# Three more leaves of a weight gradient computed by pairs, and the input sums of its fourth combination made and stored in the first convolution

## The chip, the cores and the metric

The kernel runs on one core of a Trainium2 chip. Its engines are TensorE (matmuls; PE in the profile, and PEld for the loading of its stationary operand), VectorE (DVE), ScalarE (ACT), GpSimd (POOL) and SyncE (SP). Each engine works through its own list of instructions in order. Nearly all DMAs are issued by SP, also in order. The metric is device microseconds of one execution, lower is better. The kernel before takes 1146.25 us, the median of 3 runs (1141.46 to 1150.02).

## The reference

The reference is the forward pass and the gradient of a strided convolution over time, followed by a normalization of each channel over time and a GELU:

```
B, T, D, K = 2, 16000, 256, 31          # bf16
s = 2;  L = (T - K) // s + 1            # 7985
h = sum over i < K of  x[:, i:i + s*L:s, :] @ w[i]
mu, var = mean and variance of h over time, for each channel
h = (h - mu) / sqrt(var + 1e-5) * gn_gamma + gn_beta
out = gelu(h)                           # tanh form
returns out and the gradients by x, w, gn_gamma, gn_beta for a given grad_out
```

So there are three large pieces of matmul work: the forward convolution, the gradient by x, and the gradient by w (31 matrices of 256x256, each a sum over 2 x 7985 time steps).

## The kernel before

**The five stages.** F0 and F1 are the forward convolution of the first and of the second of the two sequences (b = 0, 1), each in four chunks of time (c = 0 to 3). Beside F1, and beside the stage after it, DVE and ACT do the GELU and its derivative. G0 and G1 are the gradient by x. W is the gradient by w, the last stage, from about 818 us to the end. In F0, DVE and SP also build transposed and summed copies of w for later (`w2_part`, once in each chunk).

**Fewer products.** Every convolution is split by even and odd taps into two levels of a three-product scheme: each level replaces four products by three, at the price of sums and differences of the inputs, which DVE makes. The letters A, B_, C_ name the three branches of a level. In W the two outer levels give nine combinations, n = 0 to 8, in the order of `COMBOS`: (A,A), (A,C), (A,B), (C,B), (B,B), (B,A), (B,C), (C,A), (C,C). A letter B_ in the table means that the raw input blocks of two phases are added, so a combination with one B_ needs sums of two blocks of x, and (B,B) sums of four.

**One combination of W.** Its inputs are four tiles of x (two sequences, two phases k3; 128 partitions x 8 x 512) and tiles of the incoming gradient, which earlier stages left in DRAM (`dld`). A third level gives three leaves: the middle one, A and C_. The middle leaf is always done "by pairs", a fourth level of the same scheme: `pair_x` adds neighbouring x blocks (DVE, L1564 or L1568), `w_pairs` multiplies the sums (PE, 16 matmuls of 256 columns for each half h), `pair_d` makes two differences of the gradient (DVE, L1584), and `w_single` multiplies those by single blocks (32 matmuls of 256 columns for each half). A leaf A or C_ is done in one of two ways. If (n, leaf) is in the set `NODES`, it is done by pairs too, with `pair_x`, `pair_d` and, for each half, `w_both` (DVE, L1608), which adds the pair product to the partial sums in PSUM. Otherwise `w_leaf` does it straight: 32 matmuls of 512 columns for each half, with nothing for DVE to prepare. All matmuls of W are recorded under one line, L1498. `leaf_d` (DVE, L1669) makes the differences of the gradient for A and C_ in every combination.

**The x tiles.** There are two sets of four SBUF tiles, used by even and odd n in turn. `x_tile(n)` fills the set of combination n while n - 1 is being multiplied. Where one raw block is wanted, it is a load of 1 MB. For n = 2 and n = 4 the tiles of the two sets are added in place (`w_add`, L1463, 128x4096). For n = 3, 5 and 6 two raw blocks are to be added: the first is loaded straight into the tile, and for the other `x_more` loads two pieces of 512 KB and adds each on DVE (`w_add`, L1463, 128x2048), eight adds in one combination.

**What sets the order.** The kernel first records every operation with its dependences, and then issues all of them in the order of one long table of numbers, `SEQUENCE`, which is part of the source. So the place of an operation on its engine is given by that table, not by where it stands in the code. The table is different whenever the list of operations is.

**The buffers that matter here.** Pair sums and differences live in buffers `PD` that are used in turn: two sets for n = 2, one for n = 3 and n = 5, two for n = 8. In F0 the area of `w2_part` (`VR` and `VD`, 14 KB in each partition) holds one quarter of w at a time; its results are stored to DRAM by SP. The transposed chunk of x that F0 works on has one buffer only, so the four transposing DMAs of the next chunk (L349) can start only when the sums of the present one are made, and the next chunk's first sums on DVE (L506) wait for them.

Of the kernel before, what the change touches and what calls it, by code (L numbers as in the profile page):

```python
# [34 lines left out]
def mmt(n):  # L35
# [229 lines left out]
def conv_stem_kernel(  # L265
# [1476 lines left out]
    for b, c, br in fw:  # L1742
# [7 lines left out]
        if b == 0 and br == C_:  # L1750
            plan.hold = plan.npe
            w2_part(c)
            plan.hold = -1
# [77 lines left out]
```

## Time and profile before

| what | before |
|---|---|
| median of 3 runs | 1146.25 us (1141.46 to 1150.02) |
| the profiled execution | 1140.03 us |
| its span from first to last instruction | 1138.2 us |
| mean granted TensorE clock | 0.997 |
| PE busy | 1108.9 us, 97% |
| DVE busy | 1010.8 us, 89% |
| ACT busy | 558.7 us, 49% |
| POOL busy | 133.5 us, 12% |
| DMA | 243.56 MB, mean 214 GB/s |

The profile comes from one execution, which was 6 us below the median. In it 1.8 us lie outside the span. PE is busy nearly all of the time in every stage, with small waits for the most part; DVE is second. The views used below are the page's table of engines, the groups of instructions by line and shape, the waits, the busy time of each engine in stretches of time, and the instructions in order of time.

### The profile page before, as it was taken

What the parts mean: (1) busy time and instruction counts of PE and PEld (TensorE: products, weight loads), DVE (VectorE), ACT (ScalarE), POOL (GpSimd) and SP (SyncE); (2) the same over time, 40 slices, a digit from 0 to 9 for tenths busy, and PEclk for the clock granted to TensorE, in tenths of its full rate; (3) what the DMA queues carried; (4) which work ended last, traced back from release to release, by engine and by line L of the source; (5) the groups of instructions that cost most, each with busy time, mean ns of one, the idle gap of its engine ahead of it and who ended that gap; (6) DMA issues with size and microseconds to landing.
All of it is one profiled execution on the core that took longest, in us unless ns stands there. A gap on an engine that the chain in (4) does not pass through costs nothing. (4 is left out here: it accounts for less than half of the span.)

```text
span 1138.2 us, 18913 instructions
## 1 busy us (share of the span) xinstructions
PE 1108.9 (97%) x7592; PEld 742.6 (65%) x7592; DVE 1010.8 (89%) x1013; ACT 558.7 (49%) x826; POOL 133.5 (12%) x212
## 2 busy tenths in 40 slices
PE   7999999999999999999999999999899999999998
PEld 5888899877777974444444444444488666666785
DVE  7998687688989999899999989988999998788895
ACT  1253444487887579777867667565212212121200
POOL 0000000000000032423221332332100000000000
PEclk9999999999999999999999999999999999999999
DMA  9648827859696699999966697899997926999575
GB/s 222 97 129 137 208 84 162 202 134 214 174 229 156 202 390 250 287 262 252 265 184 173 172 224 199 196 222 229 300 292 238 299 99 191 332 328 305 187 188 144
DMA packets 358037, 243.56 MB, mean 214 GB/s; under 512 B 234167, under 2 KB 327613, under 8 KB 355773
## 3 DMA queue, kind: packets, MB, share of 16 engines
q1 hardware_dynamic: 350845, 223.47, 74.5%
q0 software_dynamic: 7104, 18.89, 5.8%
q8 instruction: 59, 0.97, 0.3%
q14 instruction: 29, 0.24, 0.1%
HBM read 106.24 MB, written 80.25 MB: 164 GB/s over the span
## 5 line engine op out<-in xcount | busy, mean ns | idle before, releaser
L548 PE MATMUL ps<-arena 128*128 128x256 bf16 (+4 forms) x3460 | 407.2, 281 | 9.9 <-DMA arena<-in_x_dram 5.2
L1232 PE MATMUL ps<-arena 128*128 128x512 bf16 (+1 forms) x1812 | 393.5, 379 | 11.5 <-DVE ps L1309 4.4
L548 PEld LDWEIGHTS <-arena 128*128 128x128 bf16 x3460 | 337.8, 98 | 79.4 <-DMA arena<-in_x_dram 5.5
L1232 PEld LDWEIGHTS <-arena 128*128 128x128 bf16 x1812 | 178.0, 98 | 225.0 <-issue 19.0
L1498 PE MATMUL ps<-arena 128*128 128x256 bf16 (+1 forms) x2320 | 309.5, 296 | 4.3 <-DMA arena<-dld 1.2
L1498 PEld LDWEIGHTS <-arena 128*128 128x128 bf16 x2320 | 226.9, 98 | 87.3 <-issue 4.1
L643 ACT ACTIVATE arena<-ps 128x1024 f32<-128x1024 f32 x124 | 125.6, 1023 | 256.9 <-PE ps L1498 83.6
L506 DVE TENSOR_TENSOR arena<-arena 128x2080 bf16<-128x2080 bf16 (+8 forms) x125 | 154.9, 1264 | 26.9 <-PE ps L548 26.3
L344 POOL DMA_DIRECT2D dld<-arena x144 | 104.0, 724 | 249.1 <-DMA arena<-arena 231.0
L923 DVE TENSOR_TENSOR arena<-arena 128x2048 bf16<-128x2048 bf16 (+1 forms) x80 | 95.5, 1196 | 6.2 <-ACT arena L917 2.6
L1463 DVE TENSOR_TENSOR arena<-arena 128x4096 bf16<-128x4096 bf16 (+1 forms) x50 | 87.3, 1772 | 6.7 <-DMA arena<-in_x_dram 3.8
L1309 DVE TENSOR_TENSOR ps<-ps,arena 128x1024 f32<-128x1024 f32 x60 | 72.3, 1225 | 8.5 <-PE ps L1232 5.3
L1180 DVE TENSOR_TENSOR arena<-arena 128x1032 bf16<-128x1032 bf16 (+1 forms) x110 | 72.0, 688 | 3.4 <-PE ps L1232 2.8
L663 ACT ACTIVATE arena<-ps 128x512 bf16<-128x512 f32 (+1 forms) x64 | 37.1, 581 | 55.9 <-PE ps L548 50.4
L1600 ACT COPY ps<-ps 128x256 f32<-128x256 f32 x54 | 19.2, 362 | 79.7 <-PE ps L1498 78.7
L353 POOL MEMSET arena<- 128x128 bf16 (+9 forms) x31 | 8.5, 297 | 403.9 <-DVE arena L506 257.6
L1319 DVE TENSOR_TENSOR arena<-ps,arena 128x1024 bf16<-128x1024 f32 x40 | 48.5, 1217 | 6.0 <-PE ps L1232 4.9
L618 ACT ACTIVATE arena<-ps 128x512 f32<-128x512 f32 x56 | 29.5, 602 | 38.6 <-PE ps L548 30.9
L1584 DVE TENSOR_TENSOR arena<-arena 128x2048 bf16<-128x2048 bf16 x36 | 43.2, 1216 | 2.8 <-PE ps L1498 2.3
L1669 DVE TENSOR_TENSOR arena<-arena 128x4608 bf16<-128x4608 bf16 x16 | 40.5, 2549 | 3.2 <-PE ps L1498 3.2
L584 ACT ACTIVATE ps<-ps 128x256 f32<-128x256 f32 x72 | 26.6, 370 | 33.5 <-PE ps L548 32.2
L913 DVE SCALAR_TENSOR_TENSOR arena<-arena 128x2048 bf16<-128x2048 bf16 (+1 forms) x16 | 35.8, 2237 | 6.7 <-ACT arena L910 6.5
(89 smaller groups left out, 791.4 us busy)
## 6 DMA issues: line engine op xcount, KB each, us to landing
arena<-in_x_dram SPq DMA_DIRECT2D x28, 1024.0 KB
dld<-arena POOLq DMA_DIRECT2D x144, 128.0 KB, 3.8
out_dram<-arena SPq DMA_DIRECT2D x31, 512.0 KB
arena<-in_x_dram SPq DMA_DIRECT2D x26, 512.0 KB
arena<-hd SPq DMA_DIRECT2D x24, 512.0 KB
arena<-dld SPq DMA_DIRECT2D x18, 640.0 KB
arena<-dld SPq DMA_DIRECT2D x18, 576.0 KB
vl<-arena SPq DMA_DIRECT2D x36, 256.0 KB
```

The costliest lines, as they stand in the source:

```text
L344: lambda: e.dma_start(out=out, in_=in_), dma=np_ * ns / 16e3 * 1.03, ns=ns, tp=SH[pk], slack=slack)
L506: lambda: nc.vector.tensor_tensor(out=o, in0=a, in1=b, op=ALU.add))
L548: yield nc.tensor.matmul(ps[:, dh, cs], lhsT=wt, rhs=mv, start=s0, stop=False, skip_group_check=True)
L643: lambda: nc.scalar.activation(out=out, in_=ps, func=ACT.Copy, scale=scale))
L923: add("DVE", dve(nf), [o], [a, b_], lambda: V.tensor_tensor(out=o, in0=a, in1=b_, op=op))
L1180: lambda: nc.vector.tensor_tensor(out=o, in0=a, in1=b, op=ALU.subtract))
L1232: yield nc.tensor.matmul(ps[:, e, 0:wide], lhsT=lt, rhs=mv, start=s0, stop=False, skip_group_check=True)
L1309: lambda ps=ps, g=g: nc.vector.tensor_tensor(out=ps[:], in0=px[:], in1=g, op=ALU.add))
L1319: lambda: nc.vector.tensor_tensor(out=ho[:, :, k, :], in0=ps[:], in1=g, op=ALU.add))
L1463: add("DVE", dve(o.free_size()), [o], [a, b], lambda: nc.vector.tensor_tensor(out=o, in0=a, in1=b, op=ALU.add))
L1498: yield nc.tensor.matmul(ps[:, s, c0:c1], lhsT=lt, rhs=mv, start=s0, stop=False, skip_group_check=True)
L1584: add("DVE", dve(2048), [o], [u, v], lambda o=o, u=u, v=v: nc.vector.tensor_tensor(out=o, in0=u, in1=v, op=ALU.subtract))
```

## The change

Two things are changed, and the order table is a new one.

First, `NODES` gains three entries: leaf A and leaf C_ of n = 2, combination (A,B), and leaf A of n = 8, combination (C,C). They are now done by pairs.

Second, the x tiles of n = 3, combination (C,B), are no longer added up in W. A new function `x_sums` does it in F0, in the first sequence's chunks 0, 1 and 2, for one, one and two of the four tiles: it loads two raw blocks in pieces of 512 KB into the area that `w2_part` uses, adds them on DVE, and stores the sum to new DRAM tiles `xs_d`. In W, `x_tile(3)` only loads them back, in two pieces of 512 KB for each tile.

```diff
 SEQUENCE = (
-    6, 11, 8, 7, 12, 5, 3, 10, 21, 15, 1, 16, 4, 2, 14, 13, 36, 34, 31, 39, 18, 30, 33, 40,
...
 )
...
+    xs_d = [[dram.tile([P, 2, 2048], BF16, name=f"xsd{b}_{k}") for k in range(2)] for b in range(NB)]
...
-    NODES = {(0, A), (0, C_), (1, A), (1, C_), (3, A), (4, A), (6, A), (7, A), (7, C_), (8, C_)}
+    NODES = {(0, A), (0, C_), (1, A), (1, C_), (3, A), (4, A), (6, A), (7, A), (7, C_), (8, C_), (2, A), (2, C_), (8, A)}
...
+    def x_sums(b, k3):
+        q = [sb(REG + 4096 * i, 4, 512) for i in range(3)]
+        for j, f in enumerate((0, 4)):
+            u, v = q[2 * j], q[1]
+            load(u, xblk(b)[:, f:f + 4, 4 * k3 + 2, :], 1 << 19, 1024)
+            load(v, xblk(b)[:, f:f + 4, 4 * k3, :], 1 << 19, 1024)
+            w_add(u, u, v)
+            load(xs_d[b][k3][:, j], u.rearrange("p f c -> p (f c)"), 1 << 19, 4096)
+
     def x_tile(n, b, k3):
...
+        elif (i1, i2) == (C_, B_):
+            for j in range(2):
+                load(t[:, 4 * j:4 * j + 4].rearrange("p f c -> p (f c)"), xs_d[b][k3][:, j], 1 << 19, 4096)
         else:
...
         if b == 0 and br == C_:
             plan.hold = plan.npe
             w2_part(c)
+            for k in ((0,), (1,), (2, 3), ())[c]:
+                x_sums(*KEYS[k])
             plan.hold = -1
```

The first place where the new order matters is DVE in combination n = 2 of W. Each row is one or more instructions in a line of the program; the line is that of the helper. In the kernel before, from the `pair_d` of the middle leaf; some rows towards the end belong to n = 3 already: L1584 is `pair_d`, L1669 `leaf_d`, L1463 `w_add` (128x4096: sums of whole tiles; 128x2048: the pieces of `x_more`), L1568 `pair_x`, L628 the last sums of n = 2.

```order
L1584 TENSOR_TENSOR arena<-arena 128x2048 x2
L1669 TENSOR_TENSOR arena<-arena 128x4608 x2
L1463 TENSOR_TENSOR arena<-arena 128x2048 x4
L1463 TENSOR_TENSOR arena<-arena 128x4096
L1584 TENSOR_TENSOR arena<-arena 128x2048 x2
L1568 TENSOR_TENSOR arena<-arena 128x2048
L1463 TENSOR_TENSOR arena<-arena 128x4096
L1463 TENSOR_TENSOR arena<-arena 128x2048 x2
L1463 TENSOR_TENSOR arena<-arena 128x4096
L1463 TENSOR_TENSOR arena<-arena 128x2048 x2
L1463 TENSOR_TENSOR arena<-arena 128x4096
L628 TENSOR_TENSOR arena<-ps,arena 128x1024 x3
```

In the changed kernel the same helpers stand some lines lower: L1684 is `leaf_d`, L1599 `pair_d`, L1583 `pair_x`, L1623 `w_both`, L1466 `w_add`, L631 the last sums.

```order
L1684 TENSOR_TENSOR arena<-arena 128x4608
L1599 TENSOR_TENSOR arena<-arena 128x2048
L1684 TENSOR_TENSOR arena<-arena 128x4608
L1583 TENSOR_TENSOR arena<-arena 128x2048 x3
L1599 TENSOR_TENSOR arena<-arena 128x2048 x3
L1623 TENSOR_TENSOR ps<-ps,arena 128x1024
L1599 TENSOR_TENSOR arena<-arena 128x2048
L1623 TENSOR_TENSOR ps<-ps,arena 128x1024 x3
L1466 TENSOR_TENSOR arena<-arena 128x4096 x2
L1583 TENSOR_TENSOR arena<-arena 128x2048
L1599 TENSOR_TENSOR arena<-arena 128x2048
L631 TENSOR_TENSOR arena<-ps,arena 128x1024
```

The eight adds of 128x2048 of `x_more` are gone from here, and `pair_x`, `pair_d` and `w_both` of the two leaves of n = 2 have come; `w_both` writes PSUM that matmuls are waiting to add to.

The second place is SP in F0, between chunk 2 and the transposing DMAs that fetch the first chunk of the second sequence. In the kernel before (`vl` are the stores of `w2_part`, `hd` that of the forward result):

```order
L344 DMA vl1_58<-arena_118 128x2x512 x2
L349 DMA_TRANSPOSE arena_118<-in_x_dram 128x8x272
L344 DMA hd0_2_62<-arena_118 128x4096
L344 DMA vl2_59<-arena_118 128x2x512
L349 DMA_TRANSPOSE arena_118<-in_x_dram 128x8x272 x3
```

In the changed kernel (`in_x_dram 128x4x512` are the loads of `x_sums`, `xsd` its stores):

```order
L347 DMA vl1_58<-arena_122 128x2x512
L347 DMA arena_122<-in_x_dram 128x4x512 x3
L347 DMA vl0_57<-arena_122 128x2x512
L347 DMA xsd1_1_101<-arena_122 128x2048
L347 DMA vl2_59<-arena_122 128x2x512
L347 DMA arena_122<-in_x_dram 128x4x512
L352 DMA_TRANSPOSE arena_122<-in_x_dram 128x8x272
L347 DMA arena_122<-in_x_dram 128x4x512 x2
L352 DMA_TRANSPOSE arena_122<-in_x_dram 128x8x272
L347 DMA xsd1_1_101<-arena_122 128x2048
L347 DMA hd0_2_62<-arena_122 128x4096
L347 DMA arena_122<-in_x_dram 128x4x512 x2
```

The loads and stores of the sums now stand before and between the four transposing DMAs of that chunk; the last two of them come after the rows shown, behind one more store of a sum, which itself waits for DVE.

287 rows, old and new, of the table SEQUENCE are left out of this document.

## The prediction

> **What bounds the kernel now.** I read the page's table and chain first, then the busy time by stretches, then the waits of PE and DVE in W, and last the groups by shape.
>
> ```profile
> span 1138.2 us, 18913 instructions
> PE 1108.9 (97%) x7592; PEld 742.6 (65%) x7592; DVE 1010.8 (89%) x1013; ACT 558.7 (49%) x826; POOL 133.5 (12%) x212
> PE 35%; DVE 4%; DMA 3%; issue 1%; ACT 0%; SPq 0%; DVEq 0%; ACTq 0%; POOLq 0%
> ```
>
> PE is idle for 29.3 us in all (1138.2 - 1108.9), and the part of the chain that could be followed is PE's in the main. So matmul time taken away counts almost in full, as long as DVE keeps up. The stretches below are, in this order, three of F0, and of W: n = 0 and 1, n = 2, n = 3, n = 4 to 6, n = 7, n = 8. Columns: length; busy us (instructions) of PE, PEld, DVE, ACT, POOL; granted clock, DMA share, GB/s.
>
> ```profile
> 60.00:100.00 40.00, 39.85 (x365) 35.45 (x363) 35.09 (x34) 19.58 (x43) 0.00 (x0) 1.00 0.62 140
> 100.00:140.00 40.00, 40.00 (x368) 35.72 (x366) 31.54 (x28) 17.09 (x39) 0.95 (x1) 1.00 0.76 168
> 140.00:200.00 60.00, 60.00 (x584) 56.86 (x582) 49.08 (x42) 29.00 (x72) 0.91 (x2) 1.00 0.55 127
> 826.00:887.40 61.40, 59.83 (x545) 53.08 (x543) 60.92 (x44) 12.79 (x19) 0.35 (x1) 1.00 0.85 258
> 887.40:925.60 38.20, 38.17 (x225) 22.00 (x226) 35.61 (x25) 5.50 (x10) 0.00 (x0) 1.00 0.61 203
> 925.60:961.50 35.90, 35.08 (x258) 24.94 (x257) 32.59 (x21) 6.76 (x11) 0.00 (x0) 1.00 0.54 174
> 961.50:1069.10 107.60, 107.60 (x736) 72.03 (x737) 92.33 (x68) 19.89 (x32) 0.00 (x0) 1.00 0.85 284
> 1069.10:1101.30 32.20, 31.59 (x289) 28.15 (x288) 29.15 (x23) 4.03 (x8) 0.00 (x0) 1.00 0.72 236
> 1101.30:1135.00 33.70, 33.23 (x242) 23.40 (x240) 25.00 (x21) 2.14 (x6) 0.53 (x1) 1.00 0.71 160
> ```
>
> In W PE is full throughout. DVE is full too in n = 0 and 1 (60.92 of 61.40) and has 2.6 us to spare in n = 2. Its slack in W is 309.0 - 275.6 = 33.4 us, and the waits, from 826 us on, say of what kind it is:
>
> ```profile
> PE ps L1498 <- DVE arena L1568: 1.1, 2, 0.6
> PE ps L1498 <- DVE ps L1608: 0.8, 2, 0.5
> PE ps L1498 <- DVE arena L628: 0.6, 1, 0.6
> PE ps L1498 <- ACT ps L1600: 0.5, 1, 0.5
> ...
> DVE arena L1527 <- PE ps L1498: 8.9, 5, 7.4
> DVE ps L1608 <- PE ps L1498: 8.5, 2, 8.0
> DVE arena L628 <- PE ps L1498: 3.2, 1, 3.2
> DVE arena L1669 <- PE ps L1498: 3.2, 1, 3.2
> ```
>
> PE waited 3.0 us in all of W, five times of six for DVE. DVE waited for PE in few long pieces, 8.0 us in n = 4 and 7.4 us near the end: there it had run ahead. So W is bound by PE with DVE close behind, and from n = 0 to n = 2 the two are level.
>
> **The change part by part.** These are the groups of W that the change touches (busy us, mean ns):
>
> ```profile
> L1498 PEld LDWEIGHTS <-arena 128*128 128x128 bf16 x2287 | 223.6, 98 | 84.8 <-issue 2.6 <-DVE arena L1568 1.7
> L1498 PE MATMUL ps<-arena 128*128 128x256 bf16 x1776 | 197.2, 273 | 3.0 <-DVE arena L1568 1.1 <-DVE ps L1608 0.8 <-DVE arena L628 0.6
> L1498 PE MATMUL ps<-arena 128*128 128x512 bf16 x512 | 112.6, 379 | 0.0
> L1584 DVE TENSOR_TENSOR arena<-arena 128x2048 bf16<-128x2048 bf16 x36 | 43.2, 1216 | 2.8 <-PE ps L1498 2.3 <-DMA out_dram<-arena 0.5
> L1568 DVE TENSOR_TENSOR arena<-arena 128x2048 bf16<-128x2048 bf16 x29 | 34.9, 1217 | 0.6 <-PE ps L1498 0.4
> L1463 DVE TENSOR_TENSOR arena<-arena 128x2048 bf16<-128x2048 bf16 x24 | 28.5, 1216 | 0.5 <-DMA arena<-in_x_dram 0.5
> L1608 DVE TENSOR_TENSOR ps<-ps,arena 128x1024 f32<-128x1024 f32 x20 | 24.1, 1224 | 8.7 <-PE ps L1498 8.5
> ```
>
> *PE.* The mean is a matmul's latency; what it takes of PE in a stream is busy time by count: 112.6/512 = 220 ns at 512 columns, 197.2/1776 = 111 ns at 256. A straight leaf is 64 of the first, 14.1 us; a leaf by pairs is 32 (`w_pairs`) and 64 (`w_single`) of the second, 10.7 us. The stretch of n = 2 checks it: 96 of 256 and 128 of 512 columns make 38.8 us, and PE was busy for 38.17, so I take 2% off. Three leaves: 3 x 3.4 x 0.98 = **10.0 us less**, all on the path.
>
> The Trainium skill speaks against such a change. In "TensorE: Matmul & The Clock Gate", section "Back-to-back issue gap", a sustained stream of weight loads and matmuls is put at about 81 ns at N = 128 and about 131 ns at N = 512, so a narrow matmul costs far more than its share. By that page, 256 columns lying by a straight line at about 98 ns (my estimate), a leaf would go from 8.4 to 9.4 us and the three leaves would cost 3 us. The trace disagrees: 220 and 111 ns, nearly the ratio of the widths.
>
> *DVE.* Consecutive instructions overlap a little, so I take what one moves the next by:
>
> ```profile
> 887.30 2.35 DVE L1584 TENSOR_TENSOR arena<-arena 128x2048 bf16<-128x2048 bf16 x2
> ...
> 889.57 5.02 DVE L1669 TENSOR_TENSOR arena<-arena 128x4608 bf16<-128x4608 bf16 x2
> ...
> 894.51 7.02 DVE L1463 TENSOR_TENSOR arena<-arena 128x2048 bf16<-128x2048 bf16 x5
> ```
>
> Two adds of 2048 take 2.27 us (889.57 - 887.30), 1.13 each, and two of 4608 take 4.94; `w_both` counts as 1.13, and an add of 4096 as 2.2, between them by size. A leaf by pairs adds two each of `pair_x`, `pair_d` and `w_both`: 6.8 us, 20.4 for three. Eight `x_more` adds leave n = 2: 9.1 us less. In W DVE has 11.3 us more to do in 10 us less: 286.9 of 299, or 96%.
>
> What PE then waits I get by adding up, along the two lists, DVE's pieces up to the last one that a matmul needs, against PE's pieces before it (16 matmuls of 256 columns as 1.75 us, of 512 as 3.45), both from the first `w_single` of n = 0. At the first `w_pairs` of n = 2 DVE was 61.5 us along and PE 59.4: 2.1 us late. In the new list it is 62.8 against 59.4, 3.4 us late, and it stays so up to the first matmul of n = 3's straight leaf (106.5 against 103.1) and to the start of n = 4. After that DVE has slack again. So DVE costs PE 1.3 us more there. In n = 7 and 8 DVE has 54.2 + 6.8 = 61.0 us of work in 65.9 - 3.3 = 62.6, with chains from the last `w_single` over a sum, `pair_d` and `w_both` (3.4 us) covered by two `w_pairs` (32 x 111 ns = 3.6 us): I take 1 us. Together **2.3 us of new waits**. The lower bound is none; the upper, all 11.3 us of DVE's work, is the first rival.
>
> *F0.* The eight adds (9.1 us of DVE) go into the first 200 us; the three stretches above leave DVE 24.3 us there. SP gets 16 loads and 8 stores of 512 KB, 12.6 MB in all. The quickest long stretch moved 284 GB/s, so that is 44 us of the DMA engines, where 0.62, 0.76 and 0.55 of their time is used in 140 us: 52 us are free. Behind the loads and stores on SP stand the next chunk's transposing DMAs, and behind these DVE's sums L506 and so PE. The cover:
>
> ```profile
> 90.84 6.98 SPq L349 DMA_TRANSPOSE arena<-in_x_dram  x2
> ...
> 102.72 1.23 DVE L506 TENSOR_TENSOR arena<-arena 128x2064 bf16<-128x2064 bf16 x1
> ...
> 172.84 11.34 SPq L349 DMA_TRANSPOSE arena<-in_x_dram  x3
> ...
> 192.60 1.23 DVE L506 TENSOR_TENSOR arena<-arena 128x2064 bf16<-128x2064 bf16 x1
> ```
>
> The last transposing DMA was issued at 97.8 and its data used at 102.7; at the next edge but one, 184.2 and 192.6. That is 4.9 and 8.4 us, less the landing. A piece of 512 KB takes 1.8 us at 284 GB/s; the order puts the pieces between the transposes, but starts chunk 2's transposes earlier in PE's work than before. I take **0.5 us**; the bounds are 0 and the second rival.
>
> *With one answer.* The x loads of n = 3 fall from 8.4 to 4.2 MB in a stretch at 203 GB/s: hidden before, hidden now, and nothing waits for them in W but the adds. The `keep` copies of n = 2 on ACT go elsewhere in the same number. The remaining waits outside W (some 25 us, with the start) belong to an order that is new everywhere; nothing says better or worse, and I give them 0 with 4 us to both sides.
>
> **Sum.** -10.0 + 2.3 + 0.5 = -7.2 us. The profiled execution (1140.03, of it 1.8 us outside the span) becomes 1132.8. It stood 6.2 us under the median, so the same step from 1146.25 gives 1139.0.
>
> **The rivals.**
>
> *DVE becomes the bound of W.* If DVE's waits for PE are the price of its order and not slack, W grows by DVE's 11.3 us rather than shrinking: 1157.6; at half of that, 1152. For it: 60.92 of 61.40 in n = 0 and 1, and n = 2 now asks 35.6 + 13.6 - 9.1 = 40.1 us of DVE for 31.5 of PE. Against: the longest wait, 8.0 us, lies in n = 4, where delayed work can go. It decides if PE's waits in n = 2 and 3 pass 7 us.
>
> *The sums' traffic holds up the transposes in F0.* This one ends slower. Chunk 0 and chunk 1 get six pieces each, chunk 2 twelve: 11, 11 and 22 us of DMA at 1.8 us. If all of it stands ahead of the transposes, the covers of 4.9, 4.9 and 8.4 us leave 6 + 6 + 13 = 25 us of PE waiting at the edges: 1146.25 - 7.7 + 25 = 1163.5. It pays for the whole gain once a third of that comes true. For it: the order of SP, pieces between the transposes of the second sequence's first chunk. Against: free DMA time, and the earlier start.
>
> *All of it, and no new wait.* The adds leave n = 2 early enough, PE's old waits shrink, the new order is better elsewhere by some us: 1146.25 - 10.0 - 3.0 = 1133.
>
> *Weight loads set the pace of narrow matmuls.* Then a pair leaf pays for 96 loads of 98 ns instead of 64: +3.1 us, 9.4 us for three, 1155.7. The trace speaks against it with 111 ns for a matmul and its load together. The rule of the Trainium skill quoted above points the same way, and by its figures the time would be 1149.
>
> *The change does nothing on the path.* That would need another engine to end W; PE's 33.23 of 33.70 us in the last stretch excludes it nearly.
>
> **How the numbers follow.** My forecast has a chance of 0.54 (1135 to 1146), all of it and more 0.24, DVE as the bound 0.11, the traffic 0.08, weight loads 0.02, nothing 0.01. The predicted time is 1139. The runs of before spread by 4 us to either side of the median, so about 1% is what can be told from no change. The range goes from 1129 (all of it, less that spread) to 1153 (DVE as the bound at half, and the edge of the traffic). Faster by over 1% is below 1134.8: 0.24 and the lower edge of the forecast, 0.28. Slower by over 1% is above 1157.7: most of the traffic, the upper end of DVE as the bound, some of the weight loads, 0.12. Within 1%: 0.60.
>
> **What would show it.** Right: in W 192 fewer matmuls of 512 columns and 288 more of 256, still near 220 and 111 ns; PE's waits in W at about 5 us, the new ones in n = 2 and 3 for L1583, L1599 or L1623; F0 without a PE wait over 1 us between 70 and 200 us. Wrong: PE waits over 7 us in n = 2 and 3 (first rival), waits on L506 or a transposing DMA at the chunk edges (second), or a 256-column matmul above 120 ns. The prediction fails as a whole if a wait outside W, made by the new order, is larger than 7 us.

## The result and the profile after

The changed kernel takes **0.9931 of the time before, 95% interval 0.9913 to 0.9949**: 1136.01 us, the median of 14 runs (1132.57 to 1141.19), against 1144.04 us (14 runs, 1141.22 to 1150.02). That is 0.7% faster, within the 1% that the forecast had as likeliest. The forecast of 1139.0 stood on a median of three runs, 1146.25, which was itself 2.2 us above the later one. The profiled execution takes 1133.30 us, of it 1131.5 in the span; before it was 1140.03. So 6.7 us are gone there, where the prediction had 7.2. The page of the kernel after:

```profile
span 1131.5 us, 19151 instructions
PE 1097.4 (97%) x7642; PEld 751.2 (66%) x7688; DVE 1029.5 (91%) x1031; ACT 557.3 (49%) x826; POOL 135.9 (12%) x212
PE 21%; DVE 10%; DMA 3%; issue 2%; SPq 1%; ACT 0%; POOL 0%; DVEq 0%; ACTq 0%; POOLq 0%
```

PE is busy for 11.5 us less, DVE for 18.7 us more, and DVE's part of the chain has gone from 4 to 10%. (46 matmul records are missing from this trace: there are 7688 weight loads and 7642 matmuls.)

To see where the time went, both spans are cut at the same events: the first matmul of F1, of G0, of W, and the end of the last matmul. The rows of stretches are, in this order, F0, F1, G0 and G1 together, W, and what comes after the last matmul; columns as in the prediction. Before:

```profile
0.00:207.64 207.64, 197.88 (x1797) 175.51 (x1797) 175.10 (x154) 82.87 (x187) 4.10 (x16) 1.00 0.68 147
207.64:412.96 205.32, 203.06 (x1607) 156.42 (x1604) 182.01 (x195) 149.07 (x233) 4.10 (x11) 1.00 0.79 204
412.96:817.63 404.67, 395.30 (x1857) 182.34 (x1858) 370.98 (x461) 274.20 (x319) 123.38 (x182) 0.99 0.92 234
817.63:1134.53 316.90, 312.64 (x2337) 228.33 (x2335) 282.31 (x205) 52.59 (x88) 1.97 (x3) 1.00 0.77 240
1134.53:1138.20 3.67, 0.00 (x1) 0.00 (x0) 0.42 (x1) 0.00 (x0) 0.00 (x0) 1.00 0.37 107
```

After:

```profile
0.00:206.68 206.68, 197.77 (x1797) 175.05 (x1798) 180.27 (x158) 80.92 (x185) 4.16 (x16) 1.00 0.83 205
206.68:418.56 211.88, 208.42 (x1659) 161.50 (x1657) 189.69 (x201) 152.28 (x245) 5.64 (x13) 1.00 0.82 210
418.56:815.88 397.32, 387.69 (x1771) 177.30 (x1805) 364.59 (x457) 271.75 (x309) 122.72 (x179) 0.99 0.90 230
815.88:1124.71 308.83, 303.49 (x2422) 237.38 (x2431) 294.56 (x216) 52.35 (x88) 3.43 (x5) 1.00 0.74 235
1124.71:1131.50 6.79, 0.00 (x0) 0.00 (x0) 0.42 (x1) 0.00 (x0) 0.00 (x0) 0.73 0.70 187
```

| stretch | before | after | difference | predicted |
|---|---|---|---|---|
| F0 | 207.64 | 206.68 | -1.0 | +0.5 |
| F1, G0, G1 together | 609.99 | 609.20 | -0.8 | 0, 4 to both sides |
| W | 316.90 | 308.83 | -8.1 | -7.7 |
| after the last matmul | 3.67 | 6.79 | **+3.1** | 0, in the 4 |
| span | 1138.2 | 1131.5 | -6.7 | -7.2 |

F1 and G are added up because the new order runs 52 more matmuls ahead of the first one of G0 (1659 against 1607); the shift between the two is only where the line falls. W does what was forecast, and the largest surprise is a tail after the last matmul that is 3.1 us longer.

W by combinations, n = 0 and 1, n = 2, n = 3, n = 4 to 6, n = 7, n = 8, after:

```profile
815.88:887.26 71.38, 67.73 (x592) 57.78 (x593) 68.84 (x52) 14.80 (x24) 2.90 (x4) 1.00 0.84 241
887.26:919.55 32.29, 31.76 (x288) 28.03 (x288) 32.29 (x25) 4.94 (x9) 0.00 (x0) 1.00 0.56 205
919.55:954.61 35.06, 34.95 (x258) 24.99 (x258) 34.99 (x23) 6.13 (x10) 0.00 (x0) 1.00 0.44 137
954.61:1062.36 107.75, 107.38 (x732) 72.00 (x737) 97.29 (x70) 20.23 (x32) 0.00 (x0) 1.00 0.91 304
1062.36:1092.24 29.88, 29.86 (x275) 26.61 (x273) 29.79 (x24) 4.11 (x8) 0.00 (x0) 1.00 0.73 238
1092.24:1124.71 32.47, 31.81 (x288) 27.96 (x286) 31.36 (x26) 2.14 (x6) 0.53 (x1) 1.00 0.51 131
```

DVE is now busy in all of n = 2 (32.29 of 32.29) and nearly all of n = 3 and n = 7. What PE waited for in W, after, and the groups of its matmuls with `w_both` (these from 824.3 us on, 8.4 us into W, as the groups of the prediction are):

```profile
PE ps L1513 <- DVE ps L1623: 1.4, 2, 1.0
PE ps L1513 <- DVE arena L1583: 1.3, 2, 0.9
PE ps L1513 <- DMA arena<-dld: 0.8, 1, 0.8
...
PE ps L1513 <- DVE arena L631: 0.3, 1, 0.3
```

```profile
L1513 PE MATMUL ps<-arena 128*128 128x256 bf16 x2064 | 228.9, 273 | 3.8 <-DVE ps L1623 1.4 <-DVE arena L1583 1.3 <-ACT arena L646 0.3
L1513 PE MATMUL ps<-arena 128*128 128x512 bf16 x311 | 69.7, 379 | 0.5
L1623 DVE TENSOR_TENSOR ps<-ps,arena 128x1024 f32<-128x1024 f32 x26 | 31.3, 1229 | 1.6 <-PE ps L1513 1.5
```

The new matmuls are there: 2064 - 1776 = 288 more of 256 columns, still 111 ns each (228.9/2064), and 320 of 512 in place of 512 (9 of their records are missing).

### The profile page after: what moved, and what is told of

It is laid out like the page before. It is cut to its first block, busy times and chain, and to the rows that moved or that the text cites. A ratio compares the mean times of both kernels' runs of the same rounds, so it can differ in the third digit from the quotient of the medians.

```text
span 1131.5 us, 19151 instructions
## 1 busy us (share of the span) xinstructions
PE 1097.4 (97%) x7642; PEld 751.2 (66%) x7688; DVE 1029.5 (91%) x1031; ACT 557.3 (49%) x826; POOL 135.9 (12%) x212
## 5 line engine op out<-in xcount | busy, mean ns | idle before, releaser
L1235 PE MATMUL ps<-arena 128*128 128x512 bf16 x1775 | 390.9, 378 | 9.7 <-ACT ps L1268 4.5
L551 PEld LDWEIGHTS <-arena 128*128 128x128 bf16 x3460 | 337.2, 98 | 82.2 <-issue 6.6
L1235 PEld LDWEIGHTS <-arena 128*128 128x128 bf16 x1812 | 178.1, 98 | 220.8 <-issue 16.8
L1513 PE MATMUL ps<-arena 128*128 128x256 bf16 (+1 forms) x2407 | 300.1, 286 | 5.2 <-DVE ps L1623 1.4
L1513 PEld LDWEIGHTS <-arena 128*128 128x128 bf16 x2416 | 235.9, 98 | 70.1 <-issue 5.4
L646 ACT ACTIVATE arena<-ps 128x1024 f32<-128x1024 f32 x126 | 126.2, 1022 | 255.2 <-PE ps L1513 103.4
L509 DVE TENSOR_TENSOR arena<-arena 128x2080 bf16<-128x2080 bf16 (+7 forms) x125 | 154.8, 1265 | 15.1 <-PE ps L551 14.4
L1466 DVE TENSOR_TENSOR arena<-arena 128x4096 bf16<-128x4096 bf16 (+1 forms) x50 | 87.9, 1775 | 7.1 <-DMA arena<-in_x_dram 6.2
L1312 DVE TENSOR_TENSOR ps<-ps,arena 128x1024 f32<-128x1024 f32 x60 | 72.5, 1227 | 6.6 <-PE ps L1235 3.5
L1599 DVE TENSOR_TENSOR arena<-arena 128x2048 bf16<-128x2048 bf16 x42 | 50.5, 1221 | 0.0
L1583 DVE TENSOR_TENSOR arena<-arena 128x2048 bf16<-128x2048 bf16 x38 | 45.5, 1220 | 0.1
L911 ACT ACTIVATE arena<-arena,stats 128x1024 bf16<-128x1024 bf16 (+1 forms) x32 | 37.9, 1212 | 8.8 <-DMA yd<-arena 8.8
```

The source lines that it names most:

```text
L509: lambda: nc.vector.tensor_tensor(out=o, in0=a, in1=b, op=ALU.add))
L551: yield nc.tensor.matmul(ps[:, dh, cs], lhsT=wt, rhs=mv, start=s0, stop=False, skip_group_check=True)
L646: lambda: nc.scalar.activation(out=out, in_=ps, func=ACT.Copy, scale=scale))
L1235: yield nc.tensor.matmul(ps[:, e, 0:wide], lhsT=lt, rhs=mv, start=s0, stop=False, skip_group_check=True)
L1312: lambda ps=ps, g=g: nc.vector.tensor_tensor(out=ps[:], in0=px[:], in1=g, op=ALU.add))
L1466: add("DVE", dve(o.free_size()), [o], [a, b], lambda: nc.vector.tensor_tensor(out=o, in0=a, in1=b, op=ALU.add))
```

## The experiments

Two theories were to be told apart from their rivals: that a leaf by pairs is 3.4 us less of PE with nothing hidden in the weight loads, and that DVE and the traffic of F0 can carry what they were given. The profile after added the question of the tail. Where it isn't edited, G takes 395 to 403 us from one profiled execution of the new order to another, while W stays between 308.4 and 309.5 us; its n = 2 to 7 repeat within 0.3 us in five of the six profiles with nothing edited in W, and are 0.5 shorter in the sixth. So the runs are compared stage by stage, above all by W.

### The changed kernel again

Nothing is edited; it is the base of the three runs that follow.

> The changed kernel once more, on the same chip as the next three, as their base. Against the kernel before: 0.993 of its time, some 8 us less by the median, 6.7 us less by the profiled executions (1131.5 and 1138.2 us of span).

Measured: 0.9942 (0.9921 to 0.9963), median 1135.93 us. Its profiled execution has a span of 1140.2, and shows what varies: W takes 308.97 us (308.83 in the first profile), the tail 6.8, but G 403.45 in place of 397.32.

### The tail

Four stores of the forward result (`out0_late`, 1024x1x256, 48x1x256 and 768x1x256 below) go ahead of the stores of n = 8's gradient (128x2x256). On SP, near the end of the program:

```diff
 L347 DMA out_dram<-arena 128x2x256 x3
-L347 DMA out_dram<-arena 1024x1x256
-L347 DMA out_dram<-arena 128x2x256
+L347 DMA out_dram<-arena 1024x1x256 x2
 L347 DMA out_dram<-arena 48x1x256
 L347 DMA out_dram<-arena 1024x1x256
-L347 DMA out_dram<-arena 128x2x256
-L347 DMA out_dram<-arena 1024x1x256
 L347 DMA out_dram<-arena 768x1x256
-L347 DMA out_dram<-arena 128x2x256 x4
+L347 DMA out_dram<-arena 128x2x256 x6
```

> The changed kernel with one thing moved: on SP the last four stores of the forward result in n = 8, whose data lay ready from 1108 us on, are put ahead of the first store of n = 8's gradient, which waits for DVE until 1118.6. Theory, the tail is the queue of stores: in the changed kernel 1.4 MB stand ahead of the last results on SP, so 6.3 us lie between the last DVE instruction (end 1125.2) and the end of the span (1131.5), where before had 3.2 (1135.0 to 1138.2). With the stores gone from there the tail is 3.2 us again, the span 3.1 us less than that of the changed kernel, and nothing else moves. Rival, the tail is the landing of the last stores themselves or the DMA engines are simply busy: the tail stays at 5 to 6.3 us and the time is the changed kernel's.

The instructions in order of time at the end of the program, in the kernel after: SP's row is the last stretch of issues without a stop, DVE's is the last sum.

```profile
1118.57 10.02 SPq L347 DMA_DIRECT2D out_dram<-arena  x12
...
1124.75 0.42 DVE L1542 TENSOR_TENSOR arena<-ps,arena 128x256 bf16<-128x256 f32 x1 [0.19 <-PE ps L1513]
```

With the stores moved:

```profile
1119.84 7.58 SPq L347 DMA_DIRECT2D out_dram<-arena  x8
...
1126.01 0.42 DVE L1542 TENSOR_TENSOR arena<-ps,arena 128x256 bf16<-128x256 f32 x1 [0.19 <-PE ps L1513]
```

In the kernel after SP is still issuing at 1128.6 (1118.57 + 10.02), 3.4 us behind the end of the last sum; with four stores fewer in that row it ends 1.0 us behind it, and the span (1129.9) ends 3.9 us behind the last matmul (1125.97) in place of 6.8. The other runs agree: 6.5 to 6.9 us in all those that have the old place of the stores, 3.7 to 4.0 in all those that have the new one or the order of before. The time is 0.991 (0.9884 to 0.9936), median 1132.23 against 1135.93 on the same chip. So the tail is the queue of stores. The gain in time is less firm: the two intervals against the kernel before overlap, and the first run of the next section, which has the stores moved too, has a median of 1136.15 on the same chip.

### Two waits of ACT in G0

The same kernel, and in G0 a copy (`g_three_b`, L1268) is moved up on ACT: by one place in the first run, in the second run by five places, and another such copy by two.

```diff
-L937 ACTIVATE arena,esum_120<-arena 128x1024
-L1268 COPY ps<-ps 128x512
-L937 ACTIVATE arena,esum_120<-arena 128x1024
+L1268 COPY ps<-ps 128x512
+L937 ACTIVATE arena,esum_120<-arena 128x1024 x2
```

> The kernel of the previous run, and at 455 us in G0 one copy of the PSUM sums on ACT (the third one of g_three_b, ready when PE ends at 454.9) put ahead of four other ACT instructions, so that the matmuls that wait for it until 460.0 can go on. Theory, a single wait of the new order costs what the profile shows: 3.5 us at 456.6 go, so with the tail 6.6 us less than the changed kernel, 1124.9 us of span. Rival, the work is only shifted: the wait comes back behind it in G0 (DVE or ACT are late there anyway), and the time is that of the previous run, 1128.4 us of span.

> The kernel of the run of the tail (the four stores moved), and in G0 two copies of PSUM sums on ACT (g_three_b) put at once behind what they wait for on PE: the one of the matmuls at 456 us ahead of five ACT instructions instead of one, and the one at 588 us ahead of two. In the run of the tail PE waited 3.9 and 0.8 us there (up to 3.2 in others), and for some 5 us behind the longer wait the granted clock read 0.5. Theory, a wait of 3.5 us and more is paid again by half a clock for 5 us (2.5 us of work), so the two places are worth up to 3.9 + 2.5 + 2 us: G (396.6 us in the run of the tail, 397 to 404 in others of the same order) comes to 391 to 395 and the time to some 1128. Rival, the waits are moved: the copies now stand ahead of other copies (keep, g_evac) that matmuls wait for next, PE waits 3 us or more in two or three pieces there, G stays at 396 or above and the time at 1132 or above.

Measured: 0.994 (0.9924 to 0.9956), median 1136.15, for the first, whose copy moved by one place only, so that the wait was still 3.07 us; 0.9889 (0.9859 to 0.992), median 1134.65, for the second, an interval that overlaps that of the run of the tail. What PE waited for in G0 in the second run, with the places moved, where the run of the tail had 4.7 us on L1268:

```profile
PE ps L1235 <- ACT ps L646: 5.1, 3, 3.0
PE ps L1235 <- ACT arena L646: 2.0, 2, 1.8
...
PE ps L1235 <- ACT ps L1268: 0.3, 1, 0.3
```

The waits for the copies are gone and waits for the next copies (`keep`, L646) are there. G takes 398.65 us, in the run of the tail 396.64. The rival holds: in G0 the waits are moved and not removed, and the 1128 of the theory did not come.

### One leaf alone

```diff
-    NODES = {(0, A), (0, C_), (1, A), (1, C_), (3, A), (4, A), (6, A), (7, A), (7, C_), (8, C_)}
+    NODES = {(0, A), (0, C_), (1, A), (1, C_), (3, A), (4, A), (6, A), (7, A), (7, C_), (8, C_), (8, A)}
```

> The kernel before with one of the three leaves alone, (8, A), by pairs; no sums are moved, the order is that of before up to n = 3 and that of the changed kernel from n = 4 on, with the four stores moved as in the run of the tail. Theory, a leaf by pairs takes 3.4 us of PE away and in n = 8 all of it is on the path: 3.4 us less than before, 1134.8 us of span, with PE busy in W 309.3 us (312.6 before). Rival, weight loads set the pace of narrow matmuls: 3.1 us more than before. Rival, DVE is the bound there: 3 x 2.27 us of new DVE work in n = 8 come back as waits of PE, and the time is that of before or 2 us above.

W and, of it, n = 7 and 8, in this run (before had 316.90 and, from 1069.13 to 1134.53, 65.40):

```profile
824.27:1139.28 315.01, 308.94 (x2356) 231.46 (x2367) 288.66 (x211) 52.50 (x88) 1.98 (x3) 1.00 0.77 242
...
1076.93:1139.28 62.35, 61.67 (x561) 54.58 (x558) 61.15 (x49) 6.25 (x14) 0.53 (x1) 1.00 0.67 196
```

n = 7 and 8 are 3.05 us shorter, with DVE busy for 61.15 of 62.35 us; PE's work in W is 308.94, as expected (309.3). The rest of W gave 1.2 us back, 0.8 of it in n = 0 and 1 (70.60 us, before 69.80), where the order is that of before. The time is 0.9982 (0.9966 to 0.9997), 2.1 us less. The leaf is worth its 3 us where it stands; both rivals fall.

### The sums alone

```diff
-    NODES = {(0, A), (0, C_), (1, A), (1, C_), (3, A), (4, A), (6, A), (7, A), (7, C_), (8, C_), (2, A), (2, C_), (8, A)}
+    NODES = {(0, A), (0, C_), (1, A), (1, C_), (3, A), (4, A), (6, A), (7, A), (7, C_), (8, C_)}
```

> The sums of n = 3 moved to the first convolution as in the changed kernel, but none of the three leaves by pairs; the order is that of the changed kernel up to the end of G0 and that of before from there on. Theory, DVE had slack and the sums alone buy nothing: W, 316.9 us in before, becomes shorter only by the waits that DVE's 9.1 us in n = 2 caused, at most 1 us; F0 costs nothing (206.7 in the changed kernel, 207.6 in before); so the time is that of before within 2 us. Rival, the relief of DVE is what made the changed kernel faster: 4 us or more less in W. Rival, the traffic in F0 has a price: F0 over 210 us.

```profile
826.01:1145.73 319.72, 312.31 (x2321) 228.07 (x2335) 273.66 (x197) 52.67 (x88) 1.97 (x3) 1.00 0.72 226
```

From the first matmul of n = 2 to the last of all, in this run, in the kernel before, and in the changed kernel:

```profile
898.63:1145.73 247.10, 244.87 (x1729) 170.45 (x1744) 205.41 (x146) 37.83 (x65) 0.53 (x1) 1.00 0.69 223
887.43:1134.53 247.10, 245.67 (x1744) 170.52 (x1744) 214.23 (x154) 38.29 (x66) 0.53 (x1) 1.00 0.73 233
887.26:1124.71 237.45, 235.76 (x1831) 179.60 (x1839) 225.72 (x165) 37.55 (x65) 0.53 (x1) 1.00 0.72 234
```

W is not shorter (319.72, before 316.90), with DVE 8.65 us emptier. From n = 2 on, where the sums were taken out, it takes 247.10 us with them and without: the sums buy nothing by themselves. The 2.8 us more lie in n = 0 and 1 (72.62, before 69.80), whose order is that of before. The time was missed: 1.0046 (1.0028 to 1.0063), 5 us more than before where at most 2 were expected. In its profile F0 is 208.5 us, and F1 and G together 617.5 where before had 610.0; there the two orders are joined. But F1 and G took 615.9 us in the run of one leaf, too, where their order is that of before. So how much of the 5 us belongs to the sums and how much to the seam can't be told from this run.

### How much DVE has to spare

Two runs go to both sides of the changed kernel. The first gives DVE in n = 2 back what the moved sums took away:

```diff
+            for f in (0, 4):
+                w_add(t[:, f:f + 4], t[:, f:f + 4], t[:, f:f + 4])
```

> The changed kernel, and in n = 2 of W eight adds more on DVE (128x2048, each x tile of n = 3 added to itself, so the values of x are doubled there and that part of the gradient is not the reference's), just ahead of n = 3's own sums: the DVE work that the moving of the sums took away, without its loads. Theory, DVE has under 1 us to spare at the start of n = 3 (its last needed instruction ends at 919.1 us, the matmul starts at 919.55): of 8 x 1.13 = 9.1 us some 8.6 come out as a wait of PE at the start of n = 3, W goes from 308.8 to 317.4. Rival, DVE runs ahead there by several us as in n = 4 of before (it idles for 14 us in W): W grows by less than 3 us.

What PE waited for from the start of n = 2 to the end of n = 3, and W:

```profile
PE ps L1515 <- DVE arena L631: 8.6, 1, 8.6
...
821.57:1141.06 319.49, 305.86 (x2422) 238.66 (x2431) 303.68 (x224) 52.33 (x88) 3.41 (x5) 0.98 0.72 228
```

The wait is 8.6 us to the tenth, at the first matmul of n = 3 as the theory had it. But W grew by 10.7 us, not 8.6; the clock in the last section has the rest. The time is 1.0029 (1.0012 to 1.0045) of before: with that work left in this place of W the change would have been a loss.

The second takes DVE's work for the two leaves of n = 2 away (their `pair_x`, `pair_d` and `w_both`):

```diff
-                pair_x(pa, lx[A])
+                if n != 2:
+                    pair_x(pa, lx[A])
```

> The changed kernel without the twelve DVE instructions that the two leaves of n = 2 by pairs need (four of pair_x, four of pair_d, four of w_both; their matmuls stay, on old data, so that part of the gradient is not the reference's): 13.6 us of DVE less in n = 2. Theory, DVE arrives just in time there and costs PE nothing: W (308.8 us in the changed kernel) becomes shorter by under 1 us. Rival, DVE is already the bound of n = 2 and 3 in the changed kernel: W becomes shorter by 3 us or more.

```profile
820.10:1127.65 307.55, 303.45 (x2432) 237.68 (x2431) 281.26 (x204) 52.33 (x88) 3.41 (x5) 1.00 0.75 237
```

W is 1.3 us shorter (a little over the 1 us expected); n = 2 and 3 have 0.6 of it (66.8 us, 67.35 in the kernel after), the rest is in n = 0 and 1, which the edit does not touch. Even the 0.6 may be scatter: the second run of the two on ACT, with nothing edited in W, has 66.72 us there. So in n = 2 DVE arrives just in time: 13.6 us less on it bring PE 0.6 us at most, 9.1 us more cost 8.6 and more. The time of this kernel, one execution, is 1136.25.

### The margin of F0

```diff
             load(xs_d[b][k3][:, j], u.rearrange("p f c -> p (f c)"), 1 << 19, 4096)
+            load(xs2_d[b][k3][:, j], u.rearrange("p f c -> p (f c)"), 1 << 19, 4096)
```

> The changed kernel, and each of the eight pieces of the sums in F0 is stored twice, the second time to another place in DRAM, right behind the first on SP: 4.2 MB more of DMA, 15 us of it at 284 GB/s, ahead of the transposing DMAs. Theory, the edges of the chunks have cover left: F0 stays at 206.7 us within 1 us. Rival, the traffic just fits: some 5 to 14 us of waits of PE at the edges of the chunks, F0 212 us or more.

F0 in this run, and two rows in order of time at the end of chunk 2 (the second is a sum of `w2_part` that waits for its transposing DMA):

```profile
0.00:215.04 215.04, 200.58 (x1796) 176.12 (x1797) 179.68 (x158) 80.88 (x185) 4.15 (x16) 0.98 0.86 214
...
151.52 0.69 DVE L498 TENSOR_TENSOR arena<-arena 128x1024 bf16<-128x1024 bf16 x1 [4.79 <-DMA arena<-in_w_dram]
```

The theory fell: F0 is 8.4 us longer than the 206.68 of the kernel after (207.2 to 208.5 in the other profiles that have its F0). The doubled stores stand on SP ahead of `w2_part`'s transposing DMAs; the sum that needs the data comes 4.8 us late, holds DVE's queue, and PE waits 4.1 us at 155.4 us for L510, a sum that stands behind it. Of the 8.4 us this wait is 4.1, and the half clock that follows it (the last section) some 2.7. The place is on the brim without the edit, too: with F0 as in the changed kernel PE waited there for 0.7 us in the run of the eight adds, 1.3 in that of the sums alone, and 1.0 in the run of 128 columns below, and not at all in the other seven. The time is 0.9988 (0.9964 to 1.0012).

### Narrow matmuls

Each of the 320 matmuls of 512 columns that are left in W is cut, in two of 256 columns or in four of 128, each piece with a weight load of its own:

```diff
-                    jobs.append((s, c0 * D, 512, xl[b][:, f, so * P:(so + 1) * P], rhs[b][:, f + c0:f + 2, :], False))
+                    for q in range(c0 * D, 512, 128):
+                        jobs.append((s, q, q + 128, xl[b][:, f, so * P:(so + 1) * P], rhs[b][:, f + q // D, q % D:q % D + 128], False))
```

> The changed kernel with each matmul of 512 columns that is left in W (320) made as two of 256 columns, with a weight load for each. Theory, a narrow matmul costs by its columns and the load is hidden: 320 x (2 x 111 - 220) ns = 0.6 us, W from 308.8 to 309.4. Rival, a load and a narrow matmul cost more than their share. The Trainium skill, page TensorE: Matmul & The Clock Gate, section Back-to-back issue gap, has 81 ns at N = 128 and 131 at N = 512 for sustained streams; by a line between them (an estimate) two of 256 cost 196 in place of 131: W would grow by 21 us, to 330.

> The changed kernel with each of the 320 matmuls of 512 columns in W made as four of 128 columns, each with its weight load. If only columns counted (55 ns each by half of the 111 ns of 256 columns), W stays at 309 us. If the load of 98 ns sets the pace where it is longer than the matmul, four take 392 ns in place of 220 and W grows by 55 us, to 364; that is the theory, and it says that 256 columns lie just above the width at which a weight load is hidden. The Trainium skill, page TensorE: Matmul & The Clock Gate, section Back-to-back issue gap, has 81 ns at N = 128: by that four take 324, against 131 at N = 512 by the same page.

W with pieces of 256 columns:

```profile
824.17:1133.25 309.08, 304.68 (x2751) 268.78 (x2751) 294.51 (x216) 52.34 (x88) 3.43 (x5) 1.00 0.74 236
```

W with pieces of 128, and its groups of loads and narrow matmuls:

```profile
815.14:1125.66 310.52, 306.26 (x3392) 277.63 (x3391) 294.63 (x216) 52.37 (x88) 3.43 (x5) 1.00 0.74 235
...
L1513 PEld LDWEIGHTS <-arena 128*128 128x128 bf16 x3358 | 274.4, 98 | 29.5 <-DVE arena L1584 2.8 <-issue 2.7 <-DVE arena L1685 0.2
...
L1513 PE MATMUL ps<-arena 128*128 128x128 bf16 x1280 | 73.0, 219 | 0.0
```

Two of 256 cost 0.2 us for all 320, or 0.7 counted from n = 2 on, where all of them stand (238.16 us against 237.45; 0.6 expected). The time is 0.9931 (0.991 to 0.9953). With four of 128 the theory of the load as the pace fell: W is 1.7 us longer, not 55 (2.3 from n = 2 on), and the one execution takes 1134.31. A matmul of 128 columns with its load takes 73.0/1280 = 57 ns, though the load alone lasts 98. The 3358 loads would make 329 us one behind the other and keep PEld busy for 274.4: the loads overlap one another as well as the matmuls. So what the prediction called hidden was right, but there is no threshold near 256 columns. The Trainium skill, "TensorE: Matmul & The Clock Gate", section "Back-to-back issue gap", has 81 ns at N = 128 and 131 at N = 512 for sustained streams of loads and matmuls; these runs have 57 and 220, and the measurement decides.

## Why the prediction was right

The range was right and so was the main term, but that the sum came so near (-7.2 us, the profiles -6.7) is in part luck: of the 2.8 us of costs that it counted 0.4 at most can be found, and a cost of 3.1 us that it did not count, the tail, stood in for them.

**PE, -10.0 us: right.** PE's work in W fell by 9.15 us (312.64 to 303.49, with some of the records missing), and W by 8.07; from n = 2 on, where the leaves are, W fell by 9.65 (247.10 to 237.45). By combinations: n = 2 and 3 took 38.20 + 35.90 = 74.1 us before and take 67.35, 6.75 less for two leaves (6.7 in the sum); n = 7 and 8 took 65.40 and take 62.35, 3.05 less for one.

**New waits of DVE, +2.3 us: not there.** The sum put 1.3 us into n = 2 to 4 and 1.0 into n = 7 and 8. In n = 2 and 3 the two leaves came out in full; in n = 7 and 8 some 0.3 us of a leaf is missing. Instead n = 0 and 1 take 71.38 us, where before (817.63 to 887.43) they took 69.80, 1.6 us more where no leaf was changed. But it is 70.6 to 72.5 us in the other profiles of the new order, and 70.60 and 72.62 in the two others whose order there is the old one (one leaf alone, the sums alone), so that can't be told from scatter. The step that failed is the adding up of DVE's and PE's pieces along the two lists: it took DVE to be 3.4 us late at the first `w_pairs` of n = 2 and to stay so. It was just in time: PE waited 0.7 us in all of n = 2 and 3, before 1.4. The margin was read rightly only by the runs on both sides of it.

**F0, +0.5 us: too small to be told, and the cover was misread.** No PE wait is longer than 0.5 us between 70 and 200 us, and F0 takes 206.7 to 208.5 us in the profiles that have the new one unedited, 207.6 and 208.4 in the two of the old. But the cover was worked out for the transposing DMAs of x (4.9 to 8.4 us), and the first to come late are those of w, whose sums stand ahead of the needed ones on DVE. There the cover is about nothing: 15 us of added DMA work cost 8.4. The 52 us of free DMA time were no cover, since the order on SP and DVE decides.

**The rest of the order, 0 with 4 us to both sides: the sign was not to be known.** F0, F1 and G gave 1.8 us in these two profiles, and the tail took 3.1. The 1.8 are scatter as far as is known: F1 and G together take 607 to 617 us in the new order, and 610.0 and 615.9 in the two profiles of the old. The tail is a term that the prediction did not name, though SP's list showed it: stores with ready data behind a store that waits. It alone took back a third of the 9.65 us that the leaves brought.

**The rivals.** DVE as the bound of W did not come, but was one step away: 9.1 us of DVE more and the change would have been slower than before. The traffic of F0 was as near. All of it and no new wait came nearly whole in W from n = 2 on, but not for the kernel, as the tail shows. Weight loads as the pace are refuted at 256 and at 128 columns.

## What to carry to other kernels

Cut two profiles at the same events and compare stage by stage before looking for a cause: a part that repeats to 0.3 us shows an effect of 1 us that the whole time, spread over 8, does not. When work is taken off the bounding engine, ask at the end of the program too what the last results queue behind: a store with ready data belongs ahead of one that waits. "Enough free time" on an engine or on the DMAs is no cover; the cover is the distance between the moment that one transfer lands and its use, at the tightest place of the queue.

## What was not expected of the hardware

**A wait of PE can be paid twice.** Stretches in order of time in the kernel after: first two behind a wait of PE of 3.46 us that ended at 416.2, then three around the end, at 460.1, of one of 3.47 us. The third number from the end is the granted clock.

```profile
416.10:418.00 1.90, 1.82 (x19) 1.79 (x19) 1.90 (x3) 1.90 (x7) 1.25 (x2) 1.00 1.00 384
418.00:420.00 2.00, 1.95 (x13) 1.06 (x12) 2.00 (x3) 1.94 (x10) 2.00 (x1) 1.00 0.96 328
...
457.00:458.86 1.86, 0.00 (x0) 0.00 (x0) 1.86 (x3) 1.86 (x3) 1.36 (x2) 1.00 1.00 361
458.86:465.68 6.82, 5.61 (x14) 2.04 (x14) 3.09 (x5) 4.80 (x8) 0.09 (x1) 0.50 1.21 293
465.68:468.00 2.32, 2.27 (x12) 1.12 (x12) 1.74 (x5) 2.32 (x3) 0.00 (x0) 1.00 1.07 349
```

And around the end, at 933.6, of the wait of 8.6 us in the run of the eight adds:

```profile
926.00:928.46 2.46, 0.00 (x0) 0.00 (x0) 2.46 (x2) 0.00 (x0) 0.00 (x0) 1.00 0.00 0
928.47:938.71 10.24, 5.09 (x25) 3.61 (x26) 10.24 (x9) 1.07 (x3) 0.00 (x0) 0.50 0.00 1
938.72:940.00 1.28, 1.28 (x13) 1.15 (x12) 1.28 (x2) 0.22 (x1) 0.00 (x0) 1.00 0.00 0
```

Of the 10.24 us at half the clock 5.1 lie behind the wait, some 2.5 us of work: n = 3 took 37.35 us there, 35.06 in the kernel after, and these 2.3 us with the 8.6 account for the 10.7. In the 13 profiles of this study, the start of the program left out, all 11 waits of 3.47 us or more were followed by half the clock, and so were 20 of the 29 waits from 2.0 to 3.46 us, for 2.6 to 6.0 us from the end of the wait. The clock record gives these stretches a length of 3.41 or 6.83 us each, 10.24 behind the longest wait, and some start before the wait ends, some up to 1.3 us behind it; the same 3.46 us at 413 us was followed by it in 8 of 11 executions. That is one reason why G, with its waits of 2 to 4 us, varies by 8 us from one execution of an order to the next and W does not: the two longest G of the new order (403.45 and 402.85 us) have 13.7 and 10.2 us at half the clock in them, the others 3.4 to 7.8. Another, the landing of its DMAs, was not followed up. The Trainium skill, "TensorE: Matmul & The Clock Gate", section "What's actually happening", says that the array falls to half its clock after an idle window of about 3.4 us that runs freely; the runs agree in kind, and in that the same wait does it at times and not at others, but here waits from 2.0 us on did it too.

**A weight load of 98 ns does not set the pace of matmuls of 128 columns**: 57 ns for a load and its matmul, above.
